# Query feature sums ahead of the second query projection, in two of the four segments

## The chip, the cores and the metric

One core of one Trainium2 chip. The metric is the device time of one execution in microseconds (us). Below, PE is the matrix engine, DVE the vector engine, ACT the scalar engine (activations), POOL the GpSimd engine, SP the engine whose queue issues most DMAs.

## The reference

Two attention layers read the same input x (2048 tokens, width 640, 32 heads of 20) and are mixed by a sigmoid gate. Layer A is a linear attention with a learned softmax feature map. Layer B, in whose code the change lies, works in four segments of 512 tokens, with a memory M, z that is carried from segment to segment:

```python
phi = lambda t: jnp.where(t > 0, t + 1.0, jnp.exp(t))
for s in range(4):
    logits = einsum('bhqd,bhkd->bhqk', qs, ks) * scale + causal_mask
    a_dot  = einsum('bhqk,bhkd->bhqd', softmax(logits), vs)
    pq     = phi(qs)
    a_mem  = einsum('bhld,bhde->bhle', pq, M) / (einsum('bhld,bhd->bhl', pq, z) + 1e-06)
    outs.append(g * a_mem + (1 - g) * a_dot)
    pk     = phi(ks)
    M, z   = M + einsum('bhld,bhle->bhde', pk, vs), z + einsum('bhld->bhd', pk)
return gate * (A @ A_wo) + (1 - gate) * (concat(outs) @ B_wo)
```

## The kernel before, in words

Layer A runs first, up to about 146 us of the profile: folded weights, projections, feature maps, its output for all tokens (kept transposed in oTA). Then layer B runs in 16 double steps, four to a segment; a double step handles two groups of four heads (steps a and b). The order on every engine is written out by hand: instructions are issued in the order in which the program emits them.

A double step has five bursts. A burst is the score matmuls of one block of keys (line 620, tile st_ps, two PSUM tiles), two exponentials on ACT (line 624, tile PT), and one or two causal masks on POOL (line 629). Between the bursts the program emits the items of the double step's string in PLAN, in order, spread by their PE time:

- **h**: one half (320 columns) of a projection of the next segment: five matmuls (line 798, tile proj) and a copy of the result by DVE (line 804). Halves come in the order k, k, q, q, v, v for one chunk of 128 tokens, so one double step does one chunk. Behind the second half of k or q, SP issues the turn: a DMA transpose (line 520) into kT or qT, from which the next segment's scores read.
- **f**: half a final output projection of a finished chunk: ten matmuls (line 749) and a copy by DVE into orow (line 760). **o** is the like for layer A's part alone.
- **y**, **x**: the feature sums of queries and of keys. Two DVE instructions build phi: a minimum on the exponential (line 777, tile ek), then max(t,0) plus it (line 778). For queries line 778 writes phiq_st (a part of the tile that the profile calls Eq), and SP then issues two DMA transposes (line 783) into unused parts of xTf, where the memory matmuls read them. The exponential (line 774) is issued on ACT earlier in the double step: for queries behind the first burst, for the chunk that the double step before projected; for keys behind the third.
- **A**, **B**: the weighted sums of values (line 672, tile nda) of query blocks 0 to 2, for step a and for the previous step b. **D**, **C**: block 3, the matmuls with the memory (line 680, reads the phi of the queries) and for its update (line 685), and the epilogue: DVE's rec (lines 697, 699), td (709), mtmp (714), then POOL's oB (711), Msb (717), Mbd (718).
- **t**: a DMA transpose of a finished output chunk (line 722).

The PSUM buffers of h, f and o come from one pool of two, so a projection can start only when DVE has copied the one before the last. PSUM for nda is a single tile. st_ps has two. The y of a segment's first double step is for the last query chunk of that same segment; the memory matmuls of D read it through the DMA.

Of the kernel before, what the change touches and what calls it, by code (L numbers as in the profile page):

```python
# [15 lines left out]
def kernel(  # L16
# [554 lines left out]
    with ExitStack() as bctx:  # L571
# [239 lines left out]
        def half_items(s, order):  # L811
# [11 lines left out]


        PLAN = {0: ("hhhhhhxAhD", "hhBhyhChoxAoD", "hoBhoyChoxAoD", "hoBooyCooxAoD"),
                1: ("hhBhhyChhxADtt", "hhBhhyCfhhxAD", "hhBhhyCfhhxADt", "hhBhhyCfhhxAD"),
                2: ("hhBhhyCfhhxADt",) * 4,
                3: ("fBfyCffADtt", "ftBfCftfAD", "fBfCftfAD", "fBfCfffAD")}

        prev = None  # L830
# [112 lines left out]
```

## Time and profile before

| | |
|---|---|
| median of 3 runs | 350.31 us (349.9 to 350.6) |
| profiled execution | 350.88 us, span 349.2 us |
| granted PE clock, mean | 0.984 |
| PE busy | 320.4 us, 92% |
| ACT busy | 260.1 us, 74% |
| DVE busy | 224.2 us, 64% |
| POOL busy | 206.3 us, 59% |
| double steps of segments two and three, first to last | 192 to 289 us of the span |

The span runs from the first to the last instruction of one profiled execution. A row of a timeline gives the start and the duration of a run of like instructions on one engine, and in brackets how long the engine stood idle before it and what ended that. A row of waits gives who waited for whom: the total in us, how many times, and the longest. In the chain of waits each row is a piece of the work that ended last.

### The profile page before, as it was taken

Reading aid. Unit: us, or ns where it says so; the run is one execution under the profiler, and the core shown is the slowest. Engines: PE = TensorE matmul, PEld = TensorE weight load, DVE = VectorE, ACT = ScalarE, POOL = GpSimd, SP = SyncE. Lnnn points to the kernel's source line nnn. Section 1 sums busy time; section 2 is a strip of 40 time slices with the busy share of each in tenths; the row PEclk is TensorE's granted clock in tenths of the full one; section 3 lists DMA queues with packets and bytes.
Section 4 is the critical chain, followed back from the end, with each engine's and each line's share of the span. In section 5 each row is a group of like instructions: output and inputs, shape, how many; then the busy total and the mean of one; then the engine's idle time right before and its main releaser. Section 6 shows DMA issues by size and latency. Waiting matters only on the chain.

```text
span 349.2 us, 9745 instructions
## 1 busy us (share of the span) xinstructions
PE 320.4 (92%) x4022; PEld 221.3 (63%) x4025; DVE 224.2 (64%) x449; ACT 260.1 (74%) x330; POOL 206.3 (59%) x300
## 2 busy tenths in 40 slices
PE   7999999999969999889988999999999999999974
PEld 6888888874437777555555566556555555666552
DVE  2466886489777889447587567765756665445423
ACT  3788887409835345699999998898888889898820
POOL 8177688500426898846565667567576667666520
PEclk9999999999989999999999999999999999999987
DMA  8839969894006778854433553743643451412102
GB/s 230 264 67 180 124 93 120 120 330 142 0 2 58 102 126 118 132 104 85 45 57 62 71 92 62 112 84 57 100 93 65 99 98 46 101 39 56 50 10 75
DMA packets 81861, 33.82 MB, mean 97 GB/s; under 512 B 67610, under 2 KB 81818, under 8 KB 81818
## 3 DMA queue, kind: packets, MB, share of 16 engines
q1 hardware_dynamic: 80954, 32.39, 50.8%
q10 hardware_dynamic: 864, 0.82, 0.8%
q8 instruction: 31, 0.51, 0.7%
q14 instruction: 12, 0.10, 0.1%
HBM read 9.21 MB, written 2.62 MB: 34 GB/s over the span
## 4 chain that ended last, share of the span: by engine, by line
PE 49%; ACT 20%; DVE 15%; issue 7%; DMA 5%; POOL 3%; SPq 0%; ACTq 0%; DVEq 0%
ACT PT L624 18%; PE st_ps L620 7%; PE pk L214 6%; PE pv L214 6%; PE proj L749 5%; PE pq L265 5%; PE proj L798 5%; PE nda L672 4%; PE proj L506 3%; DVE tt L454 2%; DVE Eq L778 2%; DVE td L709 2%; PE num L410 2%; DVE zz L251 2%; DVE rr L432 1%
## 5 line engine op out<-in xcount | busy, mean ns | idle before, releaser
L624 ACT ACTIVATE PT<-st_ps 128x1024 bf16<-128x1024 f32 x160 | 154.1, 1024 | 19.7 <-PE st_ps L620 12.3
L629 POOL TENSOR_SCALAR_AFFINE_SELECT PT<-PT 128x512 bf16<-128x512 bf16 x128 | 84.2, 675 | 53.2 <-ACT PT L624 53.0
L226 POOL TENSOR_TENSOR EkSn<-Ek,krec 128x1280 bf16<-128x1280 bf16 x16 | 37.6, 2359 | 19.0 <-DVE krec L225 17.3
L672 PEld LDWEIGHTS <-PT 128*128 128x128 bf16 x1280 | 39.7, 96 | 14.2 <-issue 7.7
L672 PE MATMUL nda<-vB,PT 128*128 128x21 bf16 x1280 | 42.8, 173 | 3.6 <-DVE td L709 1.8
L804 DVE CAST Z<-proj 128x320 bf16<-128x320 f32 x48 | 22.8, 488 | 32.5 <-PE proj L798 32.3
L798 PEld LDWEIGHTS <-xTf 128*128 128x128 bf16 x320 | 28.0, 97 | 21.4 <-issue 12.7
L214 PEld LDWEIGHTS <-xTf 128*128 128x128 bf16 x320 | 35.3, 113 | 7.1 <-ACT xTf L192 0.3
L222 DVE TENSOR_REDUCE ksum<-Ek 128x64 f32<-128x1280 bf16 x16 | 23.6, 1478 | 12.3 <-ACT Ek L218 12.3
L270 ACT ACTIVATE Eq<-pq 128x1024 bf16<-128x1024 f32 x20 | 19.4, 1021 | 14.7 <-PE pq L265 14.7
L454 DVE TENSOR_TENSOR tt<-num,rr 128x640 f32<-128x640 f32 x32 | 25.3, 815 | 6.7 <-PE num L410 4.7
L711 POOL TENSOR_TENSOR oB<-td 128x320 bf16<-128x320 f32 x24 | 20.6, 860 | 13.3 <-DVE td L709 10.5
L545 POOL TENSOR_TENSOR oA<-tt 128x640 bf16<-128x640 f32 x16 | 24.6, 1544 | 5.7 <-DVE tt L454 5.1
L620 PE MATMUL st_ps<-Z 32*128 32x512 bf16 (+3 forms) x256 | 23.4, 299 | 4.7 <-ACT PT L624 2.1
L749 PE MATMUL proj<-WkA,oTA 128*128 128x320 bf16 x160 | 27.3, 299 | 0.0
L218 ACT ACTIVATE Ek<-pk 128x640 bf16<-128x640 f32 x32 | 20.8, 701 | 7.8 <-PE pk L214 5.4
L410 PEld LDWEIGHTS <-Eq 128*128 128x128 bf16 x384 | 20.3, 96 | 9.5 <-issue 6.9
L620 PE MATMUL st_ps<-Eq 32*128 32x512 bf16 (+3 forms) x256 | 24.4, 299 | 1.8 <-ACT PT L624 1.1
L214 PE MATMUL pv<-WvA,xTf 128*128 128x321 bf16 x160 | 24.6, 300 | 0.0
L214 PE MATMUL pk<-WkA,xTf 128*128 128x320 bf16 x160 | 24.4, 299 | 0.2 <-ACT xTf L192 0.2
L265 PE MATMUL pq<-xTf,WqA 128*128 128x512 bf16 x97 | 23.4, 397 | 0.3 <-issue 0.2
L749 PE MATMUL proj<-WvA,oT 128*128 128x320 bf16 x120 | 22.6, 300 | 0.0
(137 smaller groups left out, 548.5 us busy)
## 6 DMA issues: line engine op xcount, KB each, us to landing
Z<-EkSn SPq DMA_DIRECT2D x32, 160.0 KB, 4.9
x_nat<-in_A_x_dram SPq DMA_DIRECT2D x8, 320.0 KB, 6.5
out_dram<-orow SPq DMA_DIRECT2D x10, 160.0 KB, 2.1
WvA<-in_A_wqkv_dram SPq DMA_DIRECT2D x2, 400.0 KB, 6.5
wnat_q<-in_A_wqkv_dram SPq DMA_DIRECT2D x1, 800.0 KB
WkB<-in_B_wk_dram SPq DMA_DIRECT2D x1, 800.0 KB, 7.2
WqB<-in_B_wq_dram SPq DMA_DIRECT2D x1, 800.0 KB, 9.0
WvB<-in_B_wv_dram SPq DMA_DIRECT2D x1, 800.0 KB, 10.6
```

Source lines behind the costliest of these rows:

```text
L214: nc.tensor.matmul(ps[:, bk, 0:n], lhsT=xTk[:, c, sc // 4, sc % 4], rhs=rhs, start=(c == 0), stop=(c == KC - 1))
L226: nc.gpsimd.tensor_tensor(out=EkSn[:, sc].rearrange("p s (h f) -> p (s h) f", f=DH), in0=Ek.rearrange("p s (h f) -> p (s h) f", f=DH), in1 ...
L265: nc.tensor.matmul(pq[:, half, :], lhsT=WqA[:, c, j * P:(j + 1) * P], rhs=xT[:, c, t0:t0 + 512], start=(c == 0), stop=(c == KC - 1))
L410: nc.tensor.matmul(ps(bk, lo, hi), lhsT=Eqs[qb, j][:, sgn, qc * P:(qc + 1) * P], rhs=kvx[:, sgn, j, lo - h0:hi - h0, :].rearrange("p h e - ...
L454: nc.vector.tensor_tensor(out=tt[:, sgn].rearrange("p (b h) d -> p b h d", b=2), in0=ps, in1=csb, op=ALU.mult)
L545: nc.gpsimd.tensor_tensor(out=oA.rearrange("p (h d) -> p h d", d=DH), in0=tt[:, 0], in1=tt[:, 1], op=ALU.add)
L620: nc.tensor.matmul(ps[:, i - i0, o:o + L - c * P], lhsT=kT[32 * i:32 * i + 32, c * P:(c + 1) * P], rhs=qT[32 * i:32 * i + 32, c * P:L], st ...
L624: nc.scalar.activation(out=PT[:, i0:i0 + 2], in_=ps, func=ACT.Exp, scale=SCALE_B)
L629: nc.gpsimd.affine_select(out=v, in_=v, pattern=[[0, 4], [1, P]], compare_op=ALU.is_ge, fill=0.0, base=0, channel_multiplier=-1)
L672: nc.tensor.matmul(nd[:, j, i], lhsT=block(st, c)[:, i, (j - c) * P:(j - c + 1) * P], rhs=vB[:, c, 4 * st.g + i, :], start=(c == 0), stop= ...
L749: nc.tensor.matmul(ps, lhsT=oT[:, k % KC], rhs=W[:, k % KC, hs], start=(k == 0), stop=(k == n - 1))
L798: nc.tensor.matmul(ps, lhsT=xT[:, k, sc * P:(sc + 1) * P], rhs=W[:, k, half * 320:(half + 1) * 320], start=(k == 0), stop=(k == KC - 1))
```

## The change

In the strings of the eight double steps of segments two and three (1 and 2 in the code), y stands one h further forward: between the two halves of the query projection of the chunk, and no longer behind both. Everything else is as it was.

```diff
-                1: ("hhBhhyChhxADtt", "hhBhhyCfhhxAD", "hhBhhyCfhhxADt", "hhBhhyCfhhxAD"),
-                2: ("hhBhhyCfhhxADt",) * 4,
+                1: ("hhBhyhChhxADtt", "hhBhyhCfhhxAD", "hhBhyhCfhhxADt", "hhBhyhCfhhxAD"),
+                2: ("hhBhyhCfhhxADt",) * 4,
```

In the built program, in each of the eight double steps, DVE's instructions of lines 777 and 778 for the queries now stand ahead of the copy (line 804) of the second query half, and SP's two transposes of line 783 ahead of the query turn (line 520). The orders on PE, ACT and POOL are the same.

## The prediction

> **What bounds the kernel now.** I read the page first (PE busy 320.4 of 349.2 us, ACT 260.1, DVE 224.2: no engine but PE is near full), then the windows of the eight double steps of segments two and three. Seven of them repeat every 12.1 us, with PE busy 11.3 and ACT 10.3 to 10.9, so what they cost is set by waits between engines. So I read the chain of waits there. One double step of segment two:
>
> ```profile
> 217.27 1.95 ACT PT L624 x2
> 219.26 0.39 PE st_ps L620 x4
> 219.99 0.34 issue
> 220.34 0.35 DVE ek L777
> 220.71 0.82 DVE Eq L778
> 221.53 0.28 DVE rec L697
> 222.18 0.84 DVE td L709
> 223.21 0.69 issue
> 223.90 0.37 POOL Msb L717
> 224.62 1.95 ACT PT L624 x2
> ```
>
> The two feature sums of the queries (ek L777, Eq L778) stand in the chain, between the last query projection's copy and the epilogue rec..td of the previous step. The chain then goes on over POOL to ACT. The waits of ACT and of PE over the eight double steps:
>
> ```profile
> ACT PT L624 <- POOL Mbd L718: 5.9, 7, 0.9
> PE proj L798 <- DVE orow L760: 3.7, 7, 0.5
> ```
>
> I do not take the first label. In the built program the activation's POOL wait is for the mask of the same PT buffer one double step earlier, 12 us old; its PE wait is for the score matmuls L620 just ahead. In the three timelines those begin at 224.10, and ACT starts 0.52 later (0.49 to 0.52 at the other places where ACT waits for st_ps). So PE is late, and PE is late by the second label:
>
> ```profile
> 218.33 0.49 DVE L804 CAST Z<-proj 128x320 bf16<-128x320 f32 x1 [1.26 <-PE proj L798]
> 219.93 0.49 DVE L804 CAST Z<-proj 128x320 bf16<-128x320 f32 x1 [1.10 <-PE proj L798]
> ...
> 221.45 0.35 DVE L697 RECIPROCAL rec<-nda 128x32 f32<-128x32 f32 x1
> 221.84 0.23 DVE L699 TENSOR_TENSOR rec<-rec,Eq 128x32 f32<-128x32 f32 x1
> ...
> 223.07 0.48 DVE L760 CAST orow<-proj 128x320 bf16<-128x320 f32 x1
> ```
>
> ```profile
> 220.28 0.31 PE L685 MATMUL nda<-vB,Z 128*128 128x84 bf16 x4
> ...
> 221.67 0.72 PE L749 MATMUL proj<-WvA,oT 128*128 128x320 bf16 x4
> 222.22 0.84 PE L798 MATMUL proj<-WvB,xTf 128*128 128x320 bf16 x5
> 223.60 0.57 PE L798 MATMUL proj<-WvB,xTf 128*128 128x320 bf16 x3 [0.54 <-DVE orow L760]
> 224.10 0.41 PE L620 MATMUL st_ps<-Eq 32*128 32x128 bf16 x8
> ```
>
> PE finished the output projection at 222.39, but its PSUM buffer is one of two, and DVE empties it (orow) only at 223.07, behind the sums and the epilogue. The second value projection needs that buffer and holds PE's in-order queue for 0.54.
>
> **What moves.** The built orders of PE, ACT and POOL are unchanged. On DVE, in all eight double steps, ek and Eq go ahead of the second query copy. On SP the two feature transposes (L783) that read Eq go ahead of that projection's own turn (L520). Nothing is added or removed.
>
> **DVE.** The sums read an exponential that ACT ended at 217.08, so they are ready. Behind the first query copy (start 218.33) ek begins at 218.74, Eq at 219.11, and the next instruction may start 0.74 behind Eq (221.45 less 220.71): 219.85. The second copy must wait for PE until 219.93 anyway. So the sums fit in an idle of 1.10 and cost nothing. If that cover were gone, each 0.1 delays the copy by 0.1.
>
> **Epilogue and stall.** Behind the copy, rec could start at 220.34, but it needs PE's last nda matmul, which ends 220.59: take 220.62 instead of 221.45. From rec to orow it takes 1.62: 222.24. Its projection ends at 222.39, so orow is now bound by PE, at 222.43, and ends at 222.91; PE goes on 0.05 later, as before (223.55 to 223.60), at 222.96. The first value projection ends at 223.06. So the stall goes whole, with 0.1 to spare. What is late next is ACT's own release: score matmuls at 223.56, whose second pair needs ACT's previous activation, done 223.77. That is just in time. The gain is 0.54 in six double steps and 0.47 in one: the 3.7 of the wait list.
>
> **First double step of segment two.** It has no output projection. Its chain goes Eq (198.0 to 199.2), transpose to 202.0, PE's am matmuls, which wait about 0.25 (0.57 for four where the others take 0.31). Earlier sums put that transfer more than 1 us ahead: 0.25 gained. ACT idles 0.70 behind it for PE, so it passes on.
>
> **SP.** The price of the change is here. Last double step of segment three:
>
> ```profile
> 277.55 4.58 SPq L520 DMA_TRANSPOSE Eq<-Z  x2
> 282.23 2.56 SPq L783 DMA_TRANSPOSE xTf<-Eq  x2
> ```
>
> Now the second L520 issues at 280.9 and lands 3.2 later, 284.1; the next segment's first scores (L620, all query chunks) need it at 286.59. After the change L783 starts 0.23 behind Eq's end (280.39): 280.6 to 283.2; the turn issues at 283.3 and lands at 286.5, where 286.05 is needed (286.59 less 0.54). ACT then starts 0.45 to 0.55 late; its next wait for PE, 0.18, absorbs part; PE's second score pair waits for ACT until 286.5 anyway. Loss about 0.4. At the end of segment two the same sum (turn issues 234.9, lands 3.0 later, 237.9; needed 237.7) gives 0.1. Elsewhere the turns have a segment's time. Bounds for the two together: nothing (L783 issued as fast as its least, 1.18 each) to 7.0 (below). I take 0.5, by these rows.
>
> **POOL against DVE.** Eq took 0.82 alone and 1.19 to 1.25 where a POOL mask ran beside it; L699, 0.23 alone, took up to 0.67. Eq now lies just ahead of the masks of the second burst (start 219.27, Eq 219.11), so the masks should wait and Eq not. They then end about 221.2, and L699 starts at 221.01: up to 0.2 more, still near orow's bound. Bounds: nothing, or 0.42 on Eq and 0.44 on L699. I take nothing. The Trainium skill ("SBUF — State Buffer", Who interferes with whom) says that a DVE instruction with two SBUF inputs and a GpSimd one that reads SBUF exclude each other for the whole instruction, whichever issues first. By that rule a mask that starts first (0.63) would hold Eq for up to 0.63; the 0.4 seen here lie within it.
>
> **Sum.** 3.7 + 0.25 - 0.5 = 3.45. The profiled execution took 350.88 (span 349.2), so 347.4; the median of the three runs is 350.31, 0.6 less, so 346.9. Segment four's double steps are untouched and PE-bound, and start as much earlier.
>
> **Rivals.**
> *The lock bites.* Masks get ahead of Eq and L699. Eq +0.42 puts the copy at 220.27, rec at 220.67, and with L699 +0.44 orow at 222.73, ending 223.21: PE stalls 0.2 of the 0.54. Gain 7 x 0.34 + 0.25 - 0.5 = 2.1: 348.2. For it: L699 is 0.49 or more in each second half. Against: the order at 219.1. If Eq had to wait a whole mask (0.63), 0.13 per double step is left: 0.65 in all, 349.7.
> *The turn lands late: slower.* One mechanism, at the two segment ends. L783's longest issue is 1.91 and L520's longest landing 5.3: issue at 284.4, landing 289.7, 3.65 late, 3.5 after slack. Twice that against 3.95 gives 3 us slower, 353.4. It decides from 1.97 lost at each, a landing 4.9 behind the issue. Against: these turns landed in 3.0 to 3.8, few in 4.6 or more.
> *ACT really waits for POOL* (the page's label). Mbd, held behind the masks until 222.6, would end at 224.1 instead of 224.57: 0.45 per double step, 347.4; inside the forecast's own range.
> That the change doesn't do what it says is out: the built order shows all eight moves.
>
> **Chances.** The forecast: 0.64, with a range of its own from 346.0 (nothing lost at the turns, 346.4, less half the spread of the runs shown, 349.9 to 350.6) to 347.8 (1.0 lost there, and the same half spread). Lock, 348.2: 0.2; its full form, 349.7: 0.06. Late turn: 0.1, of which 0.02 within what can be told. A measurement here can tell about 0.2%, 0.7 us. Faster by more: 0.64 + 0.2 + 0.02 of the full lock = 0.86; same: 0.04 + 0.02 = 0.06; slower 0.08. The range runs on to 349.3, the lock's 348.2 with 1.1 more lost at the turns; it leaves out the full lock and most of the late turn, and what is under 346.0.
>
> **What would show it.** In the profile after: ek and Eq between the two query copies, Eq near 0.83; the wait of proj L798 for orow near zero; ACT's 0.85 near 0.3; the period 11.6 instead of 12.1; a new wait of L620 for L520's transfer at the two segment ends, 0.1 to 0.5. Wrong, if Eq takes over 1.1 in most double steps, if orow still holds PE, or if a segment's first scores wait over 2 us.

## The result, and the profile after

| | before | after |
|---|---|---|
| median of the first comparison (6 executions each) | 350.46 us (349.72 to 351.14) | 345.88 us (344.33 to 347.51) |
| profiled execution | 350.88 us, span 349.2 | 344.33 us, span 342.6 |
| granted PE clock, mean | 0.984 | 0.993 |
| q exponential of the first double step of segment two to that of segment four | 95.54 us | 92.77 us |

The ratio is 0.987, 95% interval 0.9835 to 0.9905: faster, by 4.6 us, where 3.45 was forecast. The median lies 0.12 us under the low end of the stated range. One kernel of the experiments had executions at a lower mean clock (0.970 to 0.976) that took 4 to 5 us longer; they are left out of its time.

DVE in the changed kernel, in the double step that the prediction used (third of segment two; start, duration, and in brackets the idle time before):

```profile
214.90 0.49 DVE L804 CAST Z<-proj 128x320 bf16<-128x320 f32 x1 [1.26 <-PE proj L798]
215.31 0.32 DVE L777 TENSOR_SCALAR ek<-ek 128x640 bf16<-128x640 bf16 x1
215.66 0.82 DVE L778 SCALAR_TENSOR_TENSOR Eq<-Z,ek 128x640 bf16<-128x640 bf16 x1
216.50 0.49 DVE L804 CAST Z<-proj 128x320 bf16<-128x320 f32 x1
217.20 0.36 DVE L697 RECIPROCAL rec<-nda 128x32 f32<-128x32 f32 x1 [0.21 <-PE nda L685]
217.60 0.19 DVE L699 TENSOR_TENSOR rec<-rec,Eq 128x32 f32<-128x32 f32 x1
...
219.00 0.49 DVE L760 CAST orow<-proj 128x320 bf16<-128x320 f32 x1
```

The two sums fill the idle time between the query copies: the second copy follows without a gap, 1.60 behind the first, as before. rec now waits for PE (0.21) and not for DVE. PE there, and the waits of PE and of ACT over the eight double steps:

```profile
218.24 0.72 PE L749 MATMUL proj<-WvA,oT 128*128 128x320 bf16 x4
218.79 1.31 PE L798 MATMUL proj<-WvB,xTf 128*128 128x320 bf16 x8
220.04 0.75 PE L620 MATMUL st_ps<-Eq 32*128 32x128 bf16 x8
```

```profile
PE st_ps L620 <- ACT PT L624: 1.4, 3, 0.8
ACT PT L624 <- PE st_ps L620: 7.6, 14, 1.3
ACT PT L624 <- POOL Mbd L718: 1.3, 6, 0.2
```

The value projection's eight matmuls run through. The 3.7 us that PE waited for orow is gone from the list; of ACT's 5.9 us under the label Mbd 1.3 is left. Most double steps last 11.51 to 11.56 us instead of 12.1.

The two profiles differ by 6.6 us, and only 2.8 of these lie in the double steps. 2.7 are there before segment two starts and 1.1 from segment four on, where not one instruction was moved. The windows from 95 to 105 us of before and of after show the largest piece (column after the busy times: granted clock):

```profile
95.00:105.00 10.00, 6.52 (x79) 3.70 (x79) 7.72 (x22) 4.27 (x5) 2.08 (x5) 0.83 0.01 2
```

```profile
95.00:105.00 10.00, 7.26 (x117) 5.32 (x118) 7.61 (x19) 4.21 (x6) 2.95 (x8) 1.00 0.01 2
```

In the execution of before the clock fell there, in that of after it did not. In the other four profiles of the two kernels, shown further down, it fell too: the profile of after is the exception. So the first question was how much of the 4.6 us is the change.

### The profile page after: what moved, and what is told of

Its sections match the earlier page's. It is cut to its first block, busy times and chain, and to the rows that moved or that the text cites. A ratio compares the mean times of both kernels' runs of the same rounds, so it can differ in the third digit from the quotient of the medians.

```text
span 342.6 us, 9747 instructions
## 1 busy us (share of the span) xinstructions
PE 317.9 (93%) x4025; PEld 220.4 (64%) x4025; DVE 224.3 (65%) x449; ACT 259.6 (76%) x330; POOL 208.8 (61%) x300
## 4 chain that ended last, share of the span: by engine, by line
PE 58%; ACT 17%; DVE 12%; DMA 5%; issue 4%; POOL 1%; SPq 1%; ACTq 0%; DVEq 0%
ACT PT L624 16%; PE st_ps L620 9%; PE proj L749 8%; PE nda L672 7%; PE pk L214 6%; PE pv L214 6%; PE proj L798 6%; PE pq L265 4%; PE proj L506 3%; DVE tt L454 3%; PE num L410 2%; DMA x_nat<-in_A_x_dram 2%; DVE rr L432 2%; DVE zz L251 2%; DMA Z<-EkSn 1%
## 5 line engine op out<-in xcount | busy, mean ns | idle before, releaser
L629 POOL TENSOR_SCALAR_AFFINE_SELECT PT<-PT 128x512 bf16<-128x512 bf16 x128 | 86.6, 695 | 50.8 <-ACT PT L624 50.7
L620 PE MATMUL st_ps<-Z 32*128 32x384 bf16 (+3 forms) x256 | 24.2, 299 | 5.0 <-ACT PT L624 2.9
L265 PE MATMUL pq<-xTf,WqA 128*128 128x512 bf16 x100 | 22.1, 379 | 0.0
```

The lines of the kernel that those rows point to most:

```text
L265: nc.tensor.matmul(pq[:, half, :], lhsT=WqA[:, c, j * P:(j + 1) * P], rhs=xT[:, c, t0:t0 + 512], start=(c == 0), stop=(c == KC - 1))
L620: nc.tensor.matmul(ps[:, i - i0, o:o + L - c * P], lhsT=kT[32 * i:32 * i + 32, c * P:(c + 1) * P], rhs=qT[32 * i:32 * i + 32, c * P:L], st ...
L629: nc.gpsimd.affine_select(out=v, in_=v, pattern=[[0, 4], [1, P]], compare_op=ALU.is_ge, fill=0.0, base=0, channel_multiplier=-1)
```

## Experiments

Kernels with lines added have later line numbers (783 becomes 785, 798 becomes 800 or 804). "Double steps" is the time from the q exponential of the first double step of segment two to that of segment four, in the profiled execution. The two theories: **A**, the change frees PE of its wait for orow's buffer, about 3 us, and what exceeds that is scatter; **B**, it gains more than that, outside these segments too. Steps of the prediction have rivals of their own below.

### Both kernels again

> The changed kernel once more, unchanged. Measured first: 4.6 us faster by the medians, but in the two profiled executions segments two and three together are only 2.8 us shorter; 2.7 us were there before segment two starts. Theory A (the rest is scatter of executions: start-up loads, and the granted clock outside these segments): the gain comes out near 2.8 us, ratio 0.990 to 0.994, and the eight double steps last 92.8 us within 0.5 again. Rival B (the change itself alters the clock or the time outside the segments): ratio 0.985 to 0.989 again, with the stages ahead of segment two again 2 us or more shorter than in the kernel before.

> The kernel before, against itself, to learn how far executions of one program scatter, and in which stages. Both theories: ratio 1.000 within 0.003. A: its stages ahead of segment two differ from the first profile by up to 2 us, with the clock rows, while its eight double steps again last 95.5 us within 0.3. B: the stages ahead of segment two last as long as in the first profile, within 0.5 us.

> The kernel before once more, one look, beside the three others of this job: its double steps should last 12.0 to 12.1 us and PE's wait for orow 3.7 us in all.

> The changed kernel a third time, beside the kernel before on the same chip, for the size of the gain and the granted clock of each execution. Theory A (3 us in the eight double steps, the rest of the first 4.6 us scatter): double steps 92.7 us again; at equal granted clock the two programs differ by about 3 us. Rival B (the change also makes the rest faster): at equal granted clock they differ by 4 us or more.

| kernel, comparison | median us | ratio, 95% interval | double steps us |
|---|---|---|---|
| after, second | 345.58 | 0.9887 (0.986 to 0.9915) | 92.66 |
| after, third | 346.12 | 0.9917 (0.9884 to 0.9949) | 92.34 |
| before against itself | 349.38 | 1.0012 (0.9995 to 1.0028) | 96.14 |
| before, one look | 348.9 | none | 95.64 |

In the double steps the mean of three profiles is 95.8 before and 92.6 after: 3.2 us. Before against itself missed its mark of 95.5 within 0.3. What lies outside the double steps, in the same six profiles (us from the start of the span; the clock column is the granted clock from 95 to 105 us):

| profile | first matmul of line 190 | line 265, first to last start | clock | segment two begins | from segment four on |
|---|---|---|---|---|---|
| before, first | 9.2 | 26.7 | 0.83 | 193.4 | 60.3 |
| before against itself | 8.5 | 26.4 | 0.83 | 192.0 | 60.3 |
| before, one look | 7.9 | 26.4 | 0.83 | 191.3 | 60.3 |
| after, first | 8.3 | 25.0 | 1.00 | 190.7 | 59.2 |
| after, second | 8.3 | 26.7 | 0.83 | 192.2 | 60.0 |
| after, third | 9.4 | 26.8 | 0.83 | 193.3 | 60.0 |

Segment two begins at 192.2 on average in before and at 192.1 in after. So the 2.7 us between the first two profiles were a start 0.9 later and a dip of the clock that cost 1.7. Neither goes with the change: the two later profiles of after have the dip, and the kernel before with one instruction made twice ("Mbd twice" below) has none and takes 25.0 in that stage. Of the 1.1 from segment four on, 0.3 is seen again in the two later profiles of after; why is open.

Sorting every execution whose clock is listed: with a mean clock of 0.983 to 0.986, 33 of before have a mean of 349.6 and 10 of after 346.3; with 0.987 to 0.991, 20 have 348.8 and 5 have 345.5. At equal clock the gain is 3.3 us both times, give or take some 0.5 to 0.7 (an estimate from the scatter of single executions, 0.6 to 0.9 us), and the step of the clock alone is 0.8. All 58 of before lie between 347.8 and 351.2.

The ratios alone do not decide: 0.9887 of the second comparison lies in the band that B had named, and both intervals reach 4 us. Theory A holds by the other two readings: the stages ahead of segment two were not shorter again, and B's 4 us or more at equal clock was not seen. What makes the clock fall in one execution and not in the next stays open.

### The place on SP's queue

```diff
-   after:  y issues its two transposes (783) at once; then the turn (520)
+   turn first:   segments two and three: the transposes wait until the turn is issued
+   ends only:    that in the last double step of the two segments alone
+   turn behind:  the kernel before, DVE as it was, but the turn waits until y's transposes are issued
```

> DVE's order as in the changed kernel, but SP issues the query turn ahead of the two feature transposes, as in the kernel before. Theory A prices the SP part at the 0.8 us that PE waited at the first scores of segment three (nothing at segment four): 0.8 us faster than the changed kernel, no wait of over 0.2 us at the first scores of segments three and four, eight double steps in 92.0 us. Rival (the wait there has another cause, SP's place costs nothing): same time as the changed kernel, the 0.8 us wait stays.

> The kernel before, DVE's order unchanged, but in segments two and three SP issues the query turn behind the two feature transposes: the SP half of the change alone, with the sums still late. Turn issues about 2.6 us later, at 284.9 in the profile before, lands 288.1 at the earliest where 286.6 is needed: theory A expects 1.5 us lost at each of the two segment ends, less 0.2 slack, 2.6 us slower in all (353.0). Rival (turns are hidden anyway): same time as before.

> The changed kernel, but in the last double step of segments two and three alone SP issues the query turn ahead of the feature transposes. Theory A: the 0.4 to 0.8 us wait of PE at the first scores of segment three goes, and the first double step of segment two keeps its 0.45 us (which the kernel with every turn first lost): eight double steps in 92.2 us or a little less, 0.4 us faster than the changed kernel. Rival: the wait stays, same as the changed kernel.

The SP queue of the changed kernel at the end of segment two, then PE at the first scores of segment three:

```profile
228.07 3.50 SPq L783 DMA_TRANSPOSE xTf<-Eq  x2
231.66 1.26 SPq L520 DMA_TRANSPOSE Z<-Z  x1
```

```profile
234.84 0.40 PE L620 MATMUL st_ps<-Z 32*128 32x512 bf16 x4 [0.81 <-ACT PT L624]
```

The turn issued at 231.66 takes 3.1 to land: 234.76, and PE starts at 234.84. The label names ACT, whose last activation had ended at 234.05 (start 232.11, 1.94 long); it is the turn, as the next kernel shows. With the turn ahead, in the kernel "ends only":

```profile
226.34 4.61 SPq L520 DMA_TRANSPOSE Z<-Z  x2
231.01 2.58 SPq L785 DMA_TRANSPOSE xTf<-Eq  x2
```

```profile
235.08 0.52 PE L620 MATMUL st_ps<-Z 32*128 32x512 bf16 x4
```

PE does not wait there, and that double step lasts 11.56 us instead of 12.43 (12.01 and 11.98 in the other two profiles of after). "Ends only" has its double steps in 91.90 us, 0.7 less than the changed kernel's mean, ratio to before 0.9911 (0.9879 to 0.9942); the medians (346.13 us) cannot show so little. With every turn first they last 92.58 us where 92.0 was expected, ratio 0.9899 (0.9869 to 0.993): the end is repaired (11.56), but the first two double steps of segment two take 11.16 and 11.77 instead of 10.99 and 11.51. There the early transposes are worth 0.4, because the memory matmuls of that same double step read them: with every turn first, four of them (line 680) take 0.48 us there instead of 0.31, and PE waits 0.50 for mtmp later in it.

The turn behind, alone, is slower: 351.9 us (median of four executions), ratio 1.0072 (1.0044 to 1.0099), 1.5 to 3.5 us, where 2.6 was expected. Only its times are used here, not its profile. So the SP half of the change is a cost by itself; the early Eq pays for it.

### Another way to free the buffer

```diff
-   "hhBhhyCfhhxAD"
+   "hhBhhCfyhhxAD"      (six double steps; the first of each segment as in the changed kernel)
```

> Another way to the same end: in six of the seven double steps that PE waited in, the query sums go behind the output projection's copy (y behind f) and not ahead of the second query copy; the first double step of segments two and three is as in the changed kernel, and SP's turn stays ahead of the feature transposes in the six. Theory A (the gain is PE's wait for the PSUM buffer that orow empties, because orow's copy stands behind the sums and the epilogue): that wait is gone here too, 2.7 to 3.5 us faster than before, double steps of 11.5 to 11.8 us. Rival (the gain comes from the sums and phi being ready earlier): sums are later here than in the kernel before, so no gain, or slower.

346.57 us, ratio 0.99 (0.986 to 0.994); double steps 91.80 us, PE's wait for orow gone. The sums are later here than before the change, and the gain is that of "ends only" (91.90), which also issues the turn first at the two ends. So what counts is that the epilogue and orow's copy do not stand behind the sums; that the sums are ready earlier is worth nothing, except in the first double step. This run also separates what ACT waits for at the fifth burst. POOL, ACT and PE there:

```profile
234.76 0.73 POOL L718 CAST Mbd<-Msb 128x84 bf16<-128x84 f32 x1
```

```profile
235.02 1.94 ACT L624 ACTIVATE PT<-st_ps 128x1024 bf16<-128x1024 f32 x2 [0.21 <-PE st_ps L620]
```

```profile
234.51 0.74 PE L620 MATMUL st_ps<-Eq 32*128 32x128 bf16 x8
```

ACT starts while Mbd still runs, and 0.51 behind PE's scores, as before and after.

### Mbd twice

```diff
                 nc.gpsimd.tensor_copy(out=Mbd[:, g], in_=Msb[:, g])
+                nc.gpsimd.tensor_copy(out=Mbd[:, g], in_=Msb[:, g])
```

> The kernel before, with POOL's last copy of each epilogue (Mbd, 0.25 us) made twice. If ACT's wait at the fifth burst is for Mbd, as the list of waits names it, ACT starts 0.25 to 0.4 us later in seven double steps: 1.8 to 2.8 us slower. By the prediction's reading (ACT waits for PE's scores, PE for orow) Mbd is off the path: within 0.5 us of before.

349.85 us, ratio 1.0007 (0.9982 to 1.0031), double steps 95.94 us, inside the 95.5 to 96.1 of before. POOL's Mbd is off the path; the label "POOL Mbd" was a coincidence of times.

### The cover of the sums

```diff
-                    nc.vector.tensor_scalar_min(out=ek, in0=ek, scalar1=1.0)
+                    (three times for the queries of segments two and three, in the changed kernel)
```

> The changed kernel, with the first of the two query sums (minimum, 0.35 us) made three times in segments two and three: 0.7 us more ahead of the second query copy, to measure the cover. By the timeline after, rec waits 0.21 us for PE and orow ends about 0.15 ahead of need, so of 0.7 some 0.3 us per double step comes through to PE: 2 us slower than the changed kernel, the wait for orow back at 0.3 in seven double steps. Rival (DVE's order does not matter, only that the feature transposes are early): same as the changed kernel.

353.45 us, ratio 1.0125 (1.0087 to 1.0163): 7.3 us slower than the changed kernel, where 2 was expected. PE's wait for orow is back, 6.9 us in seven double steps. DVE and POOL in one of them, and PE in the one before (its wait is 0.94 in both):

```profile
229.77 1.35 DVE L779 TENSOR_SCALAR ek<-ek 128x640 bf16<-128x640 bf16 x3
231.16 1.13 DVE L780 SCALAR_TENSOR_TENSOR Eq<-Z,ek 128x640 bf16<-128x640 bf16 x1
...
232.99 0.52 DVE L699 TENSOR_TENSOR rec<-rec,Eq 128x32 f32<-128x32 f32 x1
```

```profile
230.31 1.30 POOL L629 TENSOR_SCALAR_AFFINE_SELECT PT<-PT 128x512 bf16<-128x512 bf16 x2 [0.98 <-ACT PT L624]
232.24 1.22 POOL L629 TENSOR_SCALAR_AFFINE_SELECT PT<-PT 128x512 bf16<-128x512 bf16 x2 [0.63 <-ACT PT L624]
```

```profile
222.53 0.57 PE L800 MATMUL proj<-WvB,xTf 128*128 128x320 bf16 x3 [0.94 <-DVE orow L760]
```

The masks now start before the sums are done. Three minima take 1.35, where three of 0.32 would take 0.96, Eq takes 1.13 instead of 0.82, L699 0.52 instead of 0.19: 1.7 us more, not 0.7. PE waits 0.94 of it, so about 0.7 is covered. This is the prediction's lock rival, brought about by force.

### Keys too

```diff
-   (turn first at the two ends)  "hhBhyhCfhhxAD"
+   (the same)                    "hhBhyhCfhxhAD"      (segment two)
```

> As the one before, and in segment two the key sums (x) also go between the two value halves, where DVE waits 1.03 us for PE. Theory A: the epilogue of step a then no longer stands behind them, and PE's wait of 0.15 us for mtmp in the double steps of segment two goes: 0.3 to 0.5 us faster than the one before, the best of all kernels here. Rival (PE's own work of 11.5 us per double step bounds it): no difference from the one before.

> The version with the turn first at the two segment ends and the key sums forward, again, beside the changed kernel: eight double steps in 91.6 us, 1.1 us less than the changed kernel's, and 0.5 to 1.5 us faster by the medians. Rival: no difference that can be measured.

DVE in the third double step of segment two:

```profile
222.02 0.49 DVE L810 CAST vB<-proj 128x320 bf16<-128x320 f32 x1 [0.19 <-PE proj L804]
222.43 0.32 DVE L778 TENSOR_SCALAR ek<-ek 128x640 bf16<-128x640 bf16 x1
222.78 0.82 DVE L779 SCALAR_TENSOR_TENSOR Z<-Z,ek 128x640 bf16<-128x640 bf16 x1
223.55 0.50 DVE L810 CAST vB<-proj 128x320 bf16<-128x320 f32 x1
```

The key sums fit between the value copies in the same way. Medians 345.39 and 345.48 us, ratios 0.9878 (0.9843 to 0.9912) and 0.9898 (0.9864 to 0.9932); double steps 91.60 us both times, 1.0 less than the changed kernel's mean. By the medians it is 0.6 us ahead of the changed kernel in the third comparison, inside the scatter: the best by the profiles, not shown by the times.

## Why the prediction was right or wrong

**The stall (3.7): right.** PE's wait for orow is gone in the first profile, and the order of things that the sum named holds: copy not delayed, rec bound by PE's last nda matmul, orow by its projection. The other way to free the buffer gave the same gain. In most double steps 12.1 became 11.51 to 11.56. In the second of segment two, though, 11.73 (12.03 and 11.74 in the other two profiles) became 11.51: in the first pair 0.2 of a wait of 0.47; why is open. Over the three profiles of each kernel, with 11.56 in place of the 12.43, 12.01 and 11.98 at the end of segment two (the turn's loss, counted below), the seven double steps gained 3.45 us.

**The first double step (0.25): right.** 11.25 to 11.40 became 10.99 in all three profiles, 0.3 us.

**The turns (0.5): the sum held, its places did not, so that it held was luck.** End of segment two: 0.1 expected, 0.4 to 0.9 lost, because the two transposes took 3.0 to 3.5 us to issue and not 2.5. End of segment three: 0.4 expected, nothing lost. SP issued right behind Eq (275.23, Eq's end 275.21) and not 0.23 later, so the turn was issued at 277.82, 2.6 behind Eq's end instead of 2.9, took 3.2 to land, as expected, and was there at 281.0; and the scores came at 281.13, 5.9 behind Eq's end, where the sum had them needed at 5.7. What holds the second transpose's issue at the end of segment two was not settled.

**The lock (nothing): right but for 0.2 to 0.4 us in one double step.** In most double steps Eq took 0.82 or 0.83 (1.21 in the first of segment two), and the masks paid: two took 1.73 instead of 1.22. L699 started at 217.60, ahead of the masks at 217.78. But in the second double step of segment three the rival showed: in the second profile of after Eq took 1.13 and L699 0.52, and PE waited 0.4 for orow; in the other two L699 took 0.65 and 0.66, and PE's eight matmuls of the value projection 1.54 and 1.56 instead of 1.31. The next double step then lasted 11.71 to 11.81; with the sums behind orow's copy L699 took 0.19 at that place and the next double step 11.51. The Trainium skill's rule ("SBUF — State Buffer", Who interferes with whom), that whichever issues first holds out the other, agrees with both: masks 0.5 longer behind Eq here, Eq 0.3 longer behind the masks in the run with three minima.

**ACT's label: right.** Two runs, the sums behind orow's copy and Mbd twice, show that Mbd is not waited for.

**The step that failed** is the last one, from the sum to the time and its range. The sum of 3.45 stands against 3.2 in the double steps and 3.3 at equal clock, so the gain was a little over-, not underestimated. But it was taken from a median of three executions, 350.31, as if that were the level of the kernel before, and the range's low end allowed half of their spread, 0.35, for it. The 58 executions of that kernel listed with the experiments have a median of 349.3, and single ones lie up to 1.9 away from it: the start of the sum lay 1.0 too high. From 349.3 the same sum gives 345.9, and 345.88 was measured. (That it fits so closely is luck: the sum is 0.2 over what the double steps gained.)

The changed kernel's first six executions were ordinary: their median is 345.88, that of the ten later ones 345.9, although four of the six had a mean clock of 0.989 or more. It was before that lay high in the first comparison, 350.46, so about 1.1 of its 4.6 us are not the change's. Its interval for the gain, 3.3 to 5.8, holds the forecast. Why that set of before lay high stays open. Sets do differ: in the three comparisons of the experiments the median of before was 349.1, 349.8 and 349.6, the first on one chip and the others on a second; on which chip the first comparison ran is not on record. None of its six executions has its clock listed; the profiled one, 350.88 us, had 0.984, at which the others average 349.6, and its start-up took 0.7 to 1.3 us longer than in the two other profiles of before. The term missing was this scatter of the starting time: with 1 us for it the range would have held the result.

## What to carry to other kernels

An instruction that is ready early belongs where its engine waits for another anyway; if it stands ahead of a copy that frees a PSUM buffer, its length shows up as a PE stall two projections later. Count what moves with it on every queue: here two DMA issues went ahead of a transfer with a deadline, a cost at a segment's end and a gain at its start. And before a prediction states a range under 1%, take the starting time from many executions and look at the granted clock row: one dip outside the changed part moved a single execution by 1.4 to 1.8 us, about half of the gain.

## What the runs showed of the hardware

- Two more minima, 0.6 us of DVE work at 0.32 each, cost 1.0 us of PE wait per double step: being late by a little put the minima, Eq and L699 beside POOL's masks, which lengthened them by 0.4, 0.3 and 0.3. The cover of a step can end with a jump.
- The list of waits named POOL's Mbd seven times, with 0.78 to 0.85 us each, though ACT waited for PE: both hung on the same run of DVE instructions (td for POOL, orow behind it for PE), at fixed distances. A run that moved the two apart showed it.
- The mean clock of executions of one program took values near 0.984 and 0.989 most often (33 and 20 of 58 of the kernel before), 0.8 us apart in time. A dip to 0.83 from 95 to 105 us made the matmuls of line 265 last 26.4 to 26.8 us instead of 25.0.
